# Five kept parts of wq instead of four, and four zero pieces moved earlier, in a two-layer decode step with its gradients

## The chip, the cores and the metric

The kernel runs on one core of a Trainium2 chip. The metric is the device time of one execution in microseconds (us). A core has five engines with their own instruction queues: PE (TensorE, matrix products; its weight loads are shown apart as PEld), DVE (VectorE), ACT (ScalarE), POOL (GpSimd) and SP (SyncE, which here does nothing but issue transfers). They work from on-chip memory (SBUF; PE writes to a second one, PSUM) and meet through semaphores. Transfers between HBM and SBUF are done by 16 DMA engines that all queues share. In this kernel SP issues every load of a weight and every store of a weight gradient (the profile's queue q1), and POOL issues the transfers that fill the untouched part of two outputs with zeros (queue q0).

## The reference, cut to what matters

One token passes through four blocks, A, B, A, B: A is attention over the last 4096 of 32768 cached keys and values (32 query heads, 4 key/value heads of 128), B is an MLP with the Mish activation. Both A blocks share the weights `wq` (1024 x 4096) and `wo` (4096 x 1024), both B blocks share `w1` (1024 x 3584) and `w2` (3584 x 1024); everything is bf16. The outputs are the result and the gradients of x, of both caches, and of all weights.

```
x = x + A(layernorm(x)); x = x + B(layernorm(x))      # twice
A(n): q = n @ wq;  p = softmax(q k^T * 128**-0.5);  return (p v) @ wo
B(n): h = n @ w1 + b1;  return mish(h) @ w2
return out, gradients of x, k_cache, v_cache, wq, wo, w1, b1, w2 for grad_out
```

As there is one token, each weight gradient is a sum of two outer products (one for each layer), 7 to 8 MiB that are computed from two short vectors each and then written. The gradients of the caches are zero outside the last 4096 positions: 56 pieces of 1 MiB of zeros. One MiB is 1.05 MB, the unit of the profile.

## The kernel before, in words

The order of the work is written out by hand; nothing is scheduled. The stages that matter, with their place in the profiled execution:

1. Forward through both layers, and backward through layer 1 (until about 245 us). Weights that don't fit are loaded again for each layer.
2. In the backward pass of attention, `attn_bwd` runs over `wo` in eight parts (the gradient of the attention output) and then over `wq` in eight parts (the gradient of the normed input; the program calls it `dn`). A part is a tile of 128 x 4096, 1 MiB. To multiply by it the other way round than it lies in memory, each of its four blocks of 128 x 1024 is turned: eight transposes on PE into PSUM (L482), and one copy back into the same place on ACT (L309) or DVE (L306), whichever is less loaded by a running count (`evac`). Then eight products with one column (L501) follow. To balance the engines, block 0 of the parts 2 to 7 isn't turned: DVE multiplies it with a broadcast vector and sums (`rowdot`, L459).
3. In layer 1's pass over `wq` (215 to 243 us), the parts named by `KEEP_Q2` stay in SBUF after they have been turned; layer 0's pass uses them again (`turned_q`), without a load and without transposes.
4. `w2`'s second pass (245 to 275 us): seven parts, each used for the MLP's output of layer 1 (`out_rows`, L347) and for the gradient of the hidden layer of layer 0.
5. `dn_b0` (275 to 285 us): the product with `w1`, which lies in SBUF (`W1`, shown as W). When it is done, W1's room is free: three slots of it are given to the ring (`ring.lend`), and other stretches take small rows that the last stage needs.
6. `attn_bwd` for layer 0: `wo` (285 to 305 us), the attention scores (305 to 315 us), `wq` (315 to 334 us).
7. The last stage (from 334 us): the weight gradients and the caches' gradients as outer products, PE into PSUM (L1063, L1114), copied to SBUF by ACT and DVE, and stored by SP in pieces of 0.375 to 1 MiB. Four outputs are filled in turns, so four buffers of 1 MiB fill at the same time; the first four may be stored by halves.

**The ring.** Streamed parts go through a ring of eight slots. The list of wanted loads is fixed at the start; `pump` issues the next one, on SP, as soon as a slot is free, and never out of order. A slot is given back by `release`, which the loops call through `later`, so that it comes after the products of the part have been issued; for `w2` that is while the next part is being worked on. A kept part of `wq` holds its slot from layer 1's pass until layer 0's. So with four kept parts, four slots serve `w2` and `wo` until `lend` adds three.

**The zeros.** `zeros(n, after)` issues n pieces from the zeroed tile `zt` on POOL. With `after`, POOL first copies one element of that tile, so the transfer cannot start before that tile is computed. Calls stand all over the backward pass, so that the zeros run beside work that doesn't fill the DMA engines; when the 56 pieces are used up, further calls do nothing. In layer 0's `attn_bwd` the hooks are `do1` (within the pass over `wo`, by part), `dp1` (after the first half of the scores), `dq1`, and `dn1` (within the pass over `wq`). `do1` at part 5 also issues small POOL transfers that put GA and GB into rows (L1025), `do1` at part 6 two more (L869); `twins` (L1055, on SP) copies rows to a second place, from which the last stage's products read.

The functions that the change touches, and what calls them:

Of the kernel before, what the change touches and what calls it, by code (L numbers as in the profile page):

```python
# [23 lines left out]
TD = D // P  # L24
# [69 lines left out]
def kernel(  # L94
# [136 lines left out]
    def want_q(k, ts=range(8)):  # L231
        for t in ts:
            ring.want(("q", k, t), wq_v[:, t, :], [P, J])

    def want_o(k, cs=range(8), homes=()):
        for c in cs:
            own = homes[c].rearrange("p (k d) -> p k d", k=4) if c < len(homes) else None
            ring.want(("o", k, c), wo_v[:, c], [P, 4, D], own, [("K", c)] if own is not None else [])
# [18 lines left out]
    def zeros(n, after=None):  # L257

        if after is not None and zjobs:
            nc.gpsimd.tensor_copy(pz[0:1, pz_n[0] % 16:pz_n[0] % 16 + 1], after[0:1, 0:1])  # L260
            pz_n[0] += 1
        for _ in range(n):
            if zjobs:
                dst = zjobs.pop()
                nc.gpsimd.dma_start(dst, zt[:])  # L265


    KEEP_Q = (5, 6, 7)
    KEEP_Q2 = (4, 5, 6, 7)
    EARLY_2 = (0, 1)  # L270
    MID_2 = (2, 3)
    W1S = W1[:].rearrange("p t f -> p (t f)")
# [17 lines left out]
    want_o(3)  # L290
    want_q(3, [t for t in range(8) if t not in KEEP_Q2])
    ring.pump()
# [4 lines left out]
    def even():  # L297
        load["D"] = load["A"] = max(load.values())
# [196 lines left out]
    def mv_open():  # L495

        fresh[0] = True
# [397 lines left out]
    def attn_bwd(l, sv, g, wo_key, wq_key, wq_keep, hooks, beside=None):  # L895
        name = f"A{l}"
        nc.vector.tensor_copy(GA[:, :, l], g[:])
        bcast(lambda c: GA[:, c, l:l + 1], TD)
        do32 = tmp([P, HQ], FP32, "da")
        mv_open()  # L900
        even()
        for c in range(8):
            ch = ring.get((*wo_key, c))

            behind[0] = max(2, 6 - max(0, c - DENSE + 1))
            rows_chunk(ch, c, GA, l, LB[0], do32, DA, 0 if c < DENSE else 1, None, (*wo_key, c))
            later(lambda c=c: ring.release((*wo_key, c)))
            hooks["do"](c)
        flush()
        for x, n0, k0 in ((0, DENSE, 0), (DENSE, 8, 1)):  # L910
            nc.vector.tensor_copy(do32[:, 4 * x:4 * n0].rearrange("p (c k) -> p c k", k=4)[:, :, k0:],
                                  TP[:, DA + 4 * x:DA + 4 * n0].rearrange("p (c k) -> p c k", k=4)[:, :, k0:])
        do_n = from_fours(do32[:])
        dov = DOC[:].rearrange("p v (g u l h) -> p v g u l h", g=G, u=2, l=2)
        do4 = do_n.rearrange("p (g h) -> p g h", g=G)
        nc.vector.tensor_copy(dov[:, 0, :, 0, l, :], do4)
        nc.gpsimd.tensor_copy(dov[:, 1, :, 1, l, :], dov[:, 0, :, 0, l, :])
        pr = small[:, 64:128]
        prv = pr[:].rearrange("p (g u h) -> p g u h", g=G, u=2)
        o4 = sv["o32"][:].rearrange("p (g h) -> p g h", g=G)  # L920
        for u in range(2):
            nc.vector.scalar_tensor_tensor(out=prv[:, :, u, :], in0=do4, scalar=float(D), in1=o4, op0=ALU.mult, op1=ALU.mult)
        sdp = small[:, 224:288]
        pxv = PX[:].rearrange("p (b l h) -> p b l h", l=2, h=8)
        dsv = DSX[:].rearrange("p (b l h) -> p b l h", l=2, h=8)
        for i in range(2):
            for t in range(16 * i, 16 * i + 16):
                for g_ in range(G):
                    c = scol(g_, t) - 512 * i
                    nc.tensor.matmul(SC[i][:, c:c + 8], lhsT=VS[:, g_, t, :],  # L930
                                     rhs=DOC[:, 0, g_ * 32 + l * 8:g_ * 32 + l * 8 + 8], start=True, stop=True)
            if i == 0:
                nc.tensor.matmul(TP[:, 320:384], lhsT=onesD[:], rhs=pr[:], start=True, stop=True)
                nc.vector.tensor_copy(sdp[:], TP[:, 320:384])
            s = SC[i].rearrange("p (tp c) -> p tp c", c=64)
            nc.vector.tensor_tensor(out=s, in0=s, in1=sdp[:, None, :].to_broadcast([P, 8, 64]), op=ALU.subtract)
            nc.vector.tensor_tensor(out=dsv[:, i * 64:(i + 1) * 64, l, :], in0=SC[i].rearrange("p (b h) -> p b h", h=8),
                                    in1=pxv[:, i * 64:(i + 1) * 64, l, :], op=ALU.mult)
        even()
        hooks["dp"]()  # L940
        dq_ps = MV[:, 320:320 + HQ]
        for i in range(2):
            for g_ in range(G):
                for t in range(16 * i, 16 * i + 16):
                    c = pcol(g_, t, l)
                    nc.tensor.matmul(dq_ps[:, g_ * 8:g_ * 8 + 8], lhsT=KT[:, g_, t, :], rhs=DSX[:, c:c + 8],
                                     start=(g_ == 0 and t == 0), stop=(t == TS - 1), skip_group_check=True)
        nc.vector.tensor_scalar(out=DQC[:, :, l], in0=dq_ps, scalar1=scale, scalar2=None, op0=ALU.mult)
        bcast(lambda c: DQC[:, c, l:l + 1], TD)
        even()  # L950
        hooks["dq"]()
        mv_open()
        bigs.append(SC[1])
        nc.vector.memset(dnp[:, 0:DENSE], 0.0)
        for t in range(TD):
            key = (*wq_key, t)
            ch = ring.get(key)
            nr = 0 if t < DENSE else 1
            behind[0] = max(2, 6 - max(0, t - DENSE + 1))
            if nr:  # L960
                rowdot(ch[:, 0:D], LB[0:1], D, dnp[:, t:t + 1])
            for k in range(nr, 4):
                h0 = 8 * k
                w = ch[:, h0 * P:(h0 + 8) * P]
                f = lambda w=w, h0=h0, t=t, k=k: mv(w, 8, TP[:, t:t + 1], lambda i: DQC[:, h0 + i, l:l + 1], k == 3)
                if key in turned_q:
                    later(f, True)
                else:
                    turned(w, 8, f)
            if t in wq_keep:  # L970
                ring.keep(key, ("q", 3, t))
                turned_q.add(("q", 3, t))
            else:
                later(lambda key=key: ring.release(key))
            hooks["dn"](t)
        flush()
        bigs.remove(SC[1])
        if beside is None:
            return ln_head(dnp, sv["n32"], sv["rstd"], g, name)
        return ln_bwd(dnp, sv["n32"], sv["rstd"], g, name, beside)  # L980

    turned_q = set()
# [13 lines left out]
    def dq3():  # L996
        zeros(3, DQC[:, 0, 1:2])

    g2 = attn_bwd(1, sA1, g3, ("o", 1), ("q", 2), KEEP_Q2,
                  dict(do=lambda c: conv(2 if 1 < c < 6 else 1), dp=dp3, dq=dq3, dn=lambda t: None),  # L1000
# [16 lines left out]
    def rowize(cols, n, base, off, queue):  # L1017

        b = big().bitcast(BF16)
        nc.tensor.transpose(b[0:2 * n, 0:P], cols[:].rearrange("p n l -> p (n l)"), ident_bf[:])  # L1020
        k = rt_n[0]
        rt_n[0] += 1
        nc.scalar.copy(rt[0:2 * n, k, :], b[0:2 * n, 0:P])
        for l in range(2):
            queue.dma_start(ROWS[base + l:base + l + 1, off:off + n * P].rearrange("o (t p) -> o t p", p=P),  # L1025
                            rt[l:2 * n:2, k, :])
# [118 lines left out]
    for c in range(7):  # L1145
        ch = ring.get(("2", 1, c))
        out_rows(ch, c, TF, lambda fb: AC[:, fb, 1:2])
        flush()
        rows_chunk(ch, c, GB, 0, LB[0], da0, DA, 2 if c else 0, "A" if c else None, ("2", 1, c))
        later(lambda c=c: ring.release(("2", 1, c)))  # L1150
        if c in (2, 4):
            zeros(1, da0[:, 4 * c:4 * c + 1])
    flush()
    bigs.remove(SC[1])
# [17 lines left out]
    def do1(c):  # L1172
        if c == 1:
            take_back("AC", 96, NOFF)
            take_back("OC", 32, NOFF)
            take_back("NB", 64, 0)
            take_back("NA", 0, 0)
        if c == 4:
            y = to_eight(YR, RT.rearrange("p a t s -> p (a t s)")[:, 0:512].bitcast(FP32))
            nc.vector.tensor_tensor(out=x4[:], in0=y, in1=x3[:], op=ALU.add)  # L1180
        if c == 5:
            rowize(GA, TD, 32, 0, nc.gpsimd)
            rowize(GB, TD, 96, 0, nc.gpsimd)
        if c == 6:
            rowize_f()

    def dp1():
        zeros(6)
        twins((96, NOFF + F), (32, NOFF + J), (64, NOFF + F))
        stage_free.extendleft(VS[:, g].rearrange("p t d -> p (t d)") for g in range(G))  # L1190

# [71 lines left out]
```

## Time and profile before

| | |
|---|---|
| median of 3 runs | 452.16 us (451.93 to 452.18) |
| profiled execution | 453.02 us, of which the span from first to last instruction is 451.2 us |
| busy: PE, PEld, DVE, ACT, POOL | 314.0, 242.7, 261.4, 209.2, 44.3 us |
| moved by DMA | 181.40 MB, mean 402 GB/s |
| of this the zeros' queue (q0) | 58.79 MB |
| of this SP's queue (q1) | 121.78 MB |

The page's rows of 40 slices (11.3 us each) give the busy share of each engine in tenths and the GB/s that the DMA engines moved. An answer by windows gives the same for chosen stretches: busy time and number of instructions of each engine, granted PE clock, DMA share and GB/s. In a timeline, a row is start, duration, engine, line, operation, tiles and count, and in brackets the idle time before it and what ended that. SPq and POOL rows with DMA_DIRECT2D are issues, not the transfers; "to landing" is the time from the issue to the last byte.

### The profile page before, as it was taken

To read this page: it belongs to the slowest core of one execution; us is meant where nothing else is said; L and a number is where in the kernel's file an instruction comes from. 1 tells how busy PE (TensorE), PEld (TensorE's weight loads), DVE (VectorE), ACT (ScalarE), POOL (GpSimd) and SP (SyncE) were. 2 spreads that over 40 slices of the span, in tenths; PEclk is the share of its full clock that TensorE was granted. 3 is DMA by queue.
4 is the path that set the end of the run, shared out by engine and by line. 5 is a ranking of instruction groups with operands and counts; after the bars stand their busy time and mean duration, and the time that the engine had idled before them with its cause. 6 is when DMAs were issued, how large, how long until landed. Compare 5 with 4: busy or idle time off the path is not lost.

```text
span 451.2 us, 12837 instructions
## 1 busy us (share of the span) xinstructions
PE 314.0 (70%) x5681; PEld 242.7 (54%) x5681; DVE 261.4 (58%) x516; ACT 209.2 (46%) x238; POOL 44.3 (10%) x95
## 2 busy tenths in 40 slices
PE   3835542556599798986797567988977888889500
PEld 3735542435576597986796455978852232235200
DVE  4504746376551663764276556773488989998400
ACT  2501101011058566772084631580448999998500
POOL 1000000000314212102100001124030000000000
PEclk9955555565559798896599956895665555555555
DMA  8999999989999999999999999998999999999995
GB/s 335 423 420 419 417 420 419 419 314 413 395 420 419 413 411 412 401 405 422 421 424 425 423 415 364 390 416 335 401 401 415 413 421 419 418 420 414 406 409 232
DMA packets 28425, 181.40 MB, mean 402 GB/s; under 512 B 3882, under 2 KB 4038, under 8 KB 9938
## 3 DMA queue, kind: packets, MB, share of 16 engines
q1 hardware_dynamic: 19862, 121.78, 66.1%
q0 software_dynamic: 8416, 58.79, 32.0%
q8 instruction: 44, 0.72, 0.6%
q14 instruction: 11, 0.09, 0.0%
q10 hardware_dynamic: 92, 0.02, 0.0%
HBM read 81.84 MB, written 98.62 MB: 400 GB/s over the span
## 4 chain that ended last, share of the span: by engine, by line
DMA 35%; PE 34%; DVE 14%; issue 5%; ACT 5%; POOL 0%; ACTq 0%; SPq 0%; DVEq 0%
DMA ring<-in_B_w_dram 13%; PE BIG L482 10%; DMA ring<-in_A_wq_dram 5%; DMA W<-in_A_wo_dram 4%; DMA out_dram<-zt 4%; DMA W<-in_B_w_dram 4%; PE TP L501 4%; PE wide L1114 4%; DVE junk L459 3%; PE BIG L660 3%; ACT ring L309 3%; DVE ring L306 3%; DMA out_dram<-KT 3%; DMA W<-in_A_k_cache_dram 2%; PE wide L1063 2%
## 5 line engine op out<-in xcount | busy, mean ns | idle before, releaser
L309 ACT COPY ring<-BIG 128x1024 bf16<-128x1024 bf16 x52 | 51.5, 1014 | 52.5 <-PE BIG L482 48.1
L1063 PE MATMUL wide<-W 2*128 2x512 bf16 x240 | 53.2, 597 | 9.0 <-ACT ring L309 2.4
L482 PE MATMUL BIG<-ident_bf,ring 128*128 128x128 bf16 x672 | 55.9, 238 | 3.2 <-issue 2.7
L482 PEld LDWEIGHTS <-ring 128*128 128x128 bf16 x768 | 53.1, 109 | 4.5 <-issue 3.9
L459 DVE CUSTOM_DVE_ANT_0 junk<-ring,SC 128x1024 bf16<-128x1024 bf16 x32 | 38.9, 1215 | 9.9 <-DMA ring<-in_B_w_dram 9.5
L1063 PEld LDWEIGHTS <-W 2*128 2x128 bf16 x240 | 12.6, 102 | 45.7 <-issue 44.6
L501 PEld LDWEIGHTS <-ring 128*128 128x128 bf16 x864 | 30.0, 98 | 12.2 <-issue 7.1
L309 ACT CAST ring<-wide 128x1024 bf16<-128x1024 f32 (+1 forms) x37 | 34.5, 1017 | 1.1 <-PE wide L1063 1.1
L265 POOL DMA_DIRECT2D out_dram<-zt x56 | 29.8, 535 | 35.2 <-DMA out_dram<-zt 34.2
L306 DVE CAST ring<-wide 128x1024 bf16<-128x1024 f32 (+1 forms) x27 | 31.3, 1198 | 2.8 <-PE wide L1063 2.8
L309 ACT COPY KT<-BIG 128x1024 bf16<-128x1024 bf16 x22 | 21.7, 1008 | 22.2 <-PE BIG L660 20.2
L306 DVE COPY ring<-BIG 128x1024 bf16<-128x1024 bf16 x32 | 21.8, 689 | 16.5 <-PE BIG L482 13.4
L459 DVE CUSTOM_DVE_ANT_0 junk<-ring,DSX 128x1024 bf16<-128x1024 bf16 x24 | 29.4, 1224 | 0.8
L482 PE MATMUL BIG<-ident_bf,W 128*128 128x128 bf16 x280 | 23.9, 234 | 1.2 <-issue 0.9
L544 PE MATMUL MV<-NA,ring 128*128 128x1 bf16 x512 | 15.1, 165 | 12.4 <-DMA ring<-in_A_wq_dram 11.0
L309 ACT COPY W<-BIG 128x1024 bf16<-128x1024 bf16 x20 | 19.8, 1016 | 7.8 <-PE BIG L482 7.7
L544 PEld LDWEIGHTS <-ring 128*128 128x128 bf16 x512 | 14.6, 103 | 13.1 <-DMA ring<-in_A_wq_dram 11.7
L1114 PE MATMUL wide<-W 32*128 32x256 bf16 x128 | 19.7, 403 | 1.5 <-DVE KT L306 0.9
L482 PEld LDWEIGHTS <-W 128*128 128x128 bf16 x288 | 19.2, 113 | 2.0 <-issue 2.0
L309 ACT CAST KT<-wide 128x1024 bf16<-128x1024 f32 x19 | 19.1, 1031 | 1.6 <-PE wide L1114 1.1
L347 PE MATMUL YR<-ring,AC 128*32 128x256 bf16 x208 | 10.6, 358 | 12.9 <-DMA ring<-in_B_w_dram 10.5
L309 ACT CAST W<-wide 128x1024 bf16<-128x1024 f32 x16 | 16.0, 1025 | 6.6 <-PE wide L1063 6.2
(280 smaller groups left out, 527.0 us busy)
## 6 DMA issues: line engine op xcount, KB each, us to landing
out_dram<-zt POOLq DMA_DIRECT2D x56, 1024.0 KB, 20.0
ring<-in_A_wq_dram SPq DMA_DIRECT2D x24, 1024.0 KB, 13.2
ring<-in_A_wo_dram SPq DMA_DIRECT2D x14, 1024.0 KB, 19.6
ring<-in_B_w_dram SPq DMA_DIRECT2D x13, 1024.0 KB, 19.7
W<-in_A_wo_dram SPq DMA_DIRECT2D x10, 1024.0 KB, 15.9
out_dram<-ring SPq DMA_DIRECT2D x8, 1024.0 KB, 13.9
W<-in_B_w_dram SPq DMA_DIRECT2D x8, 896.0 KB, 17.7
W<-in_A_k_cache_dram SPq DMA_DIRECT2D x4, 1024.0 KB, 9.0
```

The costliest lines, as they stand in the source:

```text
L265: nc.gpsimd.dma_start(dst, zt[:])
L306: nc.vector.tensor_copy(dst, src)
L309: nc.scalar.copy(dst, src)
L347: nc.tensor.matmul(bank[32 * j:32 * j + 32, 0:n].rearrange("p (g a) -> p g a", a=m.shape[-1]), lhsT=vec.to_broadcast([P, 32]), rhs=m, star ...
L459: nc.vector.tensor_tensor_reduce(out=out, in0=a, in1=vec, scale=1.0, scalar=acc if i else 0.0, op0=ALU.mult, op1=ALU.add, accum_out=acc)
L482: nc.tensor.transpose(b[:, i * P:(i + 1) * P], block(w, i) if block else w[:, i * P:(i + 1) * P], ident_bf[:])
L501: nc.tensor.matmul(out, lhsT=w[:, i * P:(i + 1) * P], rhs=rhs_of(i), start=fresh[0], stop=last and i == n - 1, skip_group_check=True)
L544: nc.tensor.matmul(q_ps[:, h:h + 1], lhsT=ch[:, h * P:(h + 1) * P], rhs=NA[:, t, l:l + 1], start=(k == 0 and h == 0), stop=(k == TD - 1), ...
L660: nc.tensor.transpose(b[:, i * P:(i + 1) * P], T[:, g, 8 * b8 + i, :], ident_bf[:])
L1063: nc.tensor.matmul(b[:, 512 * i:512 * i + 512], lhsT=R[at:at + 2, lo:lo + P], rhs=R[at:at + 2, ro + 512 * i:ro + 512 * i + 512], start=Tru ...
L1114: nc.tensor.matmul(b[:, k * 256:(k + 1) * 256], lhsT=RT[32 * g:32 * g + 32, a, tp, :], rhs=YS[32 * g:32 * g + 32, :], start=True, stop=Tru ...
```

## The change

`KEEP_Q2` gets part 3 as well, so five parts stay in the ring between layer 1's pass over `wq` and layer 0's, and layer 0 loads three parts. Layer 0's pass takes kept and loaded parts in turns (3, 0, 4, 1, 5, 2, 6, 7 instead of 0 to 7; layer 1's order is as before, as nothing is kept then); its hooks count steps, not parts. `w2`'s pass issues one piece of zeros at parts 1, 2, 4 and 5 instead of 2 and 4. `do1` at part 5 issues two pieces after its small transfers, and `dp1` four instead of six. As there are 56 pieces in all, the last call, after layer 0's `wq` pass (`zeros(2, ...t2)`), finds none left.

```diff
-    KEEP_Q2 = (4, 5, 6, 7)
+    KEEP_Q2 = (3, 4, 5, 6, 7)
...
-        for t in range(TD):
+        kept = [t for t in range(TD) if (*wq_key, t) in turned_q]
+        got = [t for t in range(TD) if t not in kept]
+        order = [x for i in range(TD) for x in kept[i:i + 1] + got[i:i + 1]]
+        for i, t in enumerate(order):
             key = (*wq_key, t)
             ch = ring.get(key)
             nr = 0 if t < DENSE else 1
...
-            hooks["dn"](t)
+            hooks["dn"](i)
...
-        if c in (2, 4):
+        if c in (1, 2, 4, 5):
             zeros(1, da0[:, 4 * c:4 * c + 1])
...
         if c == 5:
             rowize(GA, TD, 32, 0, nc.gpsimd)
             rowize(GB, TD, 96, 0, nc.gpsimd)
+            zeros(2)
...
     def dp1():
-        zeros(6)
+        zeros(4)
```

## The prediction

> **What bounds the kernel now.** I read the page's slices first, then the same by chosen stretches, then the DMA queues and the timelines of SP and POOL. The slices:
>
> ```profile
> DMA  8999999989999999999999999998999999999995
> GB/s 335 423 420 419 417 420 419 419 314 413 395 420 419 413 411 412 401 405 422 421 424 425 423 415 364 390 416 335 401 401 415 413 421 419 418 420 414 406 409 232
> ```
>
> The DMA engines are busy from end to end, at about 415 GB/s, with a few dips. By stretches:
>
> ```profile
> core 0: us, PE busy (x) PEld busy (x) DVE busy (x) ACT busy (x) POOL busy (x), PEclk, DMA share, GB/s
> 228.60:250.00 21.40, 17.95 (x425) 16.56 (x423) 15.72 (x33) 13.34 (x14) 0.71 (x2) 1.00 1.01 424
> 250.00:275.00 25.00, 15.64 (x269) 12.51 (x265) 12.82 (x24) 11.56 (x12) 1.48 (x5) 0.67 1.01 417
> 275.00:280.00 5.00, 4.86 (x100) 3.62 (x100) 4.12 (x12) 0.00 (x0) 1.17 (x3) 0.58 0.95 300
> 280.00:305.00 25.00, 21.14 (x437) 19.84 (x430) 18.13 (x43) 15.89 (x18) 5.55 (x10) 0.93 1.02 405
> 305.00:310.00 5.00, 4.05 (x131) 3.90 (x129) 1.93 (x9) 0.00 (x0) 3.42 (x7) 0.65 0.68 259
> 310.00:338.00 28.00, 23.93 (x497) 20.93 (x495) 16.60 (x30) 10.19 (x12) 6.09 (x15) 0.62 1.01 400
> 338.00:424.00 86.00, 73.77 (x395) 26.46 (x393) 76.54 (x76) 80.39 (x90) 0.00 (x0) 0.50 1.01 416
> 424.00:446.40 22.40, 0.00 (x0) 0.00 (x0) 0.00 (x0) 0.52 (x1) 0.00 (x0) 0.50 1.00 400
> ```
>
> From 424 to 446.4 us no engine works and the stores still drain at 400 GB/s. So the end is set by bytes: all that must be moved, plus the time in which the DMA engines had too little to do. Two such holes lie near the change: 275 to 280 us (300 GB/s) and 305 to 310 us (259 GB/s).
>
> How the two queues share, by queue in windows: the first two rows are 230 to 250 us, the third is 310 to 330 us, the last is from the first store, 338.3 us, to 360 us.
>
> ```profile
> q0 software_dynamic: 584, 4.22, 50.4%
> q1 hardware_dynamic: 577, 4.20, 50.0%
> ...
> q0 software_dynamic: 1081, 7.86, 98.4%
> ...
> q0 software_dynamic: 677, 4.87, 54.3%
> ```
>
> With zeros and loads both waiting, each gets half: 4.2 MB in 20 us, 5.0 us for a piece of 1.05 MB. Alone, zeros get everything. At the first store 4.87 MB of zeros are still to be moved.
>
> **The change part by part.**
>
> *One load less.* 1.05 MB at the 417 GB/s of 250 to 275 us: 2.5 us off the bytes.
>
> *Three slots for w2.* SP's issues:
>
> ```profile
> 228.64 6.40 SPq L71 DMA_DIRECT2D ring<-in_B_w_dram  x4
> 249.84 6.09 SPq L71 DMA_DIRECT2D ring<-in_B_w_dram  x3
> 261.65 13.12 SPq L71 DMA_DIRECT2D ring<-in_A_wo_dram  x4
> 280.24 1.72 SPq L71 DMA_DIRECT2D W<-in_A_wo_dram  x3
> 292.07 4.47 SPq L71 DMA_DIRECT2D ring<-in_A_wq_dram  x3
> 297.70 0.33 SPq L71 DMA_DIRECT2D W<-in_A_wq_dram  x1
> ```
>
> The chain, and the waits of PE in the pass:
>
> ```profile
> 234.71 19.52 DMA ring<-in_B_w_dram
> 254.28 0.62 PE YR L347 x16
> 255.60 13.85 DMA ring<-in_B_w_dram
> 269.49 1.04 PE YR L347 x12
> ...
> PE YR L347 <- DMA ring<-in_B_w_dram: 7.2, 4, 3.6
> ```
>
> Parts 0 to 3 of w2 are issued by 234.7 us into the four free slots; 4 to 6 wait for the release of 0 to 2, from 249.84 us on. PE waits for each of parts 3 to 6, 7.2 us in sum, so this pass already runs at the pace of its loads. With three slots, part 3 takes the issue at 249.84 us, 15 us later, and each later load moves back by one release. Zeros hold the other half of the DMA time, so part 3 needs 5.0 us of transfer plus a start. The start isn't shown alone; I bound it by 1 us and by 4 us (a lone zero piece, below, lands 6.6 us after its issue, of which 2.5 us is its transfer), and take 2 us, as SP's issue needs less than POOL's. Part 3 then lands at 256.8 us instead of 254.3: 2.5 us late (1.5 to 4.5). Before, parts 3 to 6 were 15.2 us apart in all, 5.1 us each, which is the half rate already; I add 0.5 us for the thinner queue. The pass ends 3.0 us later.
>
> *Two more zeros beside w2's pass.* 2.1 MB are now moved ahead of the last parts of `wo`: 5.1 us, less the hole at 275 to 280 us, which they fill: (417 - 300) x 5 / 417 = 1.4 us. So the last part of `wo` lands 3.7 us later; PE is busy for 21.14 of 25 us there, so the pass has little to wait with. I take 3.5 us for the end of the pass over `wo` (1.5 to 6). Behind it on POOL nothing waits: its next issues need ACT's copies.
>
> *Two zeros from dp1 to wo's part 5.* POOL:
>
> ```profile
> 299.01 2.06 POOL L1025 DMA_DIRECT2D W<-W  x4 [14.86 <-ACT W L1023]
> 303.20 1.00 POOL L869 DMA_DIRECT2D W<-W  x2 [2.13 <-ACT W L867]
> 306.77 3.21 POOL L265 DMA_DIRECT2D out_dram<-zt  x6
> ```
>
> Before, nothing big is issued between the last load of `wq` (297.7 us) and the zeros at 306.77 us; the loads run out and leave the hole at 305 to 310 us. Two pieces issued after the first row fill it: (414 - 259) x 5 / 414 = 1.9 us. The L869 transfers now queue behind 2.1 MB; `twins` waits for them on SP, but DQC's rows, next on SP, only come with DQC, about 13 us later.
>
> *The pass over wq.* It loses three turned blocks: 24 transposes, three copies, no product.
>
> ```profile
> 315.70:334.70 19.00, 15.72 (x326) 15.24 (x325) 12.15 (x22) 7.63 (x9) 3.33 (x10) 0.68 1.02 405
> L482 PE MATMUL BIG<-ident_bf,ring 128*128 128x128 bf16 x72 | 7.5, 277 | 1.0 <-issue 1.0
> 333.11 1.22 DVE L459 CUSTOM_DVE_ANT_0 junk<-ring,SC 128x1024 bf16<-128x1024 bf16 x1
> 316.12 2.08 SPq L1025 DMA_DIRECT2D W<-W  x2
> 322.77 3.19 SPq L1055 DMA_DIRECT2D W<-W  x2
> W<-W SPq DMA_DIRECT2D x4, 9.0 KB, 6.2
> ```
>
> 24 of 72 transposes are 2.5 us of PE's 7.5, and the order in turns spreads DVE's dots, whose last ends the pass now. But the last stage's first product reads the second copy of DQC's rows, issued until 326.0 us and landing 6.2 us later, at 332.2 us, against 334.7 us when the stage starts now. So the gain is between 0 and 2.5 us; I take the middle, 1.2. The last stage starts 3.5 - 1.2 = 2.3 us later.
>
> *The end.* Stores in the last stage:
>
> ```profile
> 338.30 2.94 SPq L1040 DMA_DIRECT2D out_dram<-W  x3
> 342.80 4.24 SPq L1035 DMA_DIRECT2D out_dram<-W  x3
> 350.75 0.33 SPq L1035 DMA_DIRECT2D out_dram<-ring  x1
> ```
>
> ACT and DVE make 166 copies in 86 us, 0.52 us each, up to 256 KiB a copy. The first four buffers go out early, 3.9 MiB (4.1 MB); the next four are full after 32 copies, at about 353 us with the small work between. From 338.3 to 353 us the DMA engines could move 14.7 x 0.414 = 6.1 MB, so 2.0 MB of zeros must bridge it. Afterwards copies (39.85 MB in some 90 us) outrun the DMA engines.
>
> *The sum,* against the profiled 453.0 us. By bytes: 453.0 - 2.5 - 1.4 - 1.9 + 0.5 (w2's thinner queue) = 447.7. Zeros left at 338.3 us: 4.87 - 1.05 - (1.4 + 1.9 - 0.5) x 0.414 = 2.65 MB; at the new first store, 2.3 us later, 1.7 MB: 0.3 MB too few, 0.7 us. **448.4 us.** The same from the other side: first store 340.6 + bridge 2.0 / 0.414 = 4.8 + stores 39.85 / 0.414 = 96.3 + 6.7 from the last transfers to the end (453.0 - 446.3) = 448.4. The profiled execution is 0.9 us above the median, so 447.5 us.
>
> **A rule weighed.** Landing of POOL's zeros, first those issued at 275.2 us, then those at 306.8 us:
>
> ```profile
> DMA to landing us min/median/max: 10.2/12.5/14.9
> ...
> DMA to landing us min/median/max: 6.6/11.8/17.3
> ```
>
> Both met DMA engines with time to spare, but beside a DVE that is busy 4.12 of 5 us the first piece took 10.2 us, beside one busy 1.93 of 5 us 6.6 us. The Trainium skill, SBUF — State Buffer, section "SBUF: two separate sides", says that a DMA issued from GpSimd gets its descriptors late while DVE holds the port they share, and only appears to be blocked. The trace fits that without proving it; what it would do here is the second rival.
>
> **The rivals.**
>
> 1. *The delay wins (slower).* With three slots only two loads are in flight; if each needs the 13.85 us of the chain's last one, parts come 6.9 us apart instead of 5.1: 4 x 1.8 = 7.2, with part 3's 2.5 us 9.7 us late, and the last stage 8.5 us late. Once zeros run out the time is 446.1 us plus this delay, so it decides from 6.9 us on; at 8.5 us it is 454.6, 453.7 against the median. For it: the four waits. Against it: those 13.85 us are mostly time in queue behind other loads, which three slots shorten.
> 2. *The holes stay.* Zeros moved beside a busy DVE start 3.6 us later (10.2 - 6.6) and miss the holes of 5 us. Only the load counts: 453.0 - 2.5 + 0.5 = 451.0, 450.1 against the median. Against it: the added zeros at w2's parts stand in a queue that isn't empty.
> 3. *It cancels.* The mechanism of the first with a delay of 6 to 7.8 us: 452.1 to 453.9, the time of before.
>
> **How the numbers follow.** Forecast 0.54 (446 to 450), first rival 0.21, second 0.17, third 0.08. Faster takes the forecast and the second: 0.71 and a little of the third, 0.72; 0.2% is about what a measurement here can tell from no change. The low end is the bytes with both holes filled and nothing new, 453.0 - 5.8 - 0.9 = 446.3, and 0.3 for zeros that mix with loads (424 GB/s, not 400): 446.0. The high end cuts off the worst half of the first rival: 453.7.
>
> **What would show it.** DMA moved about 180.35 MB; part 3 of w2 issued near 250 us; no slice under 390 GB/s from 275 to 310 us; the pass over `wo` ending near 308.5 us, the last stage starting near 337 us; less than 2 MB of zeros beside the first stores. The prediction is wrong if the last stage starts after 341 us, or if a hole of more than 2 us opens in w2's pass.

## The result, and the profile after

The changed kernel takes 451.35 us (median of 20 runs, 449.92 to 453.25) where the kernel before takes 452.35 us (20 runs, 451.63 to 454.07): a ratio of 0.9979, 95% interval 0.9969 to 0.9989. A second set gave 451.06 us and 0.9972 (0.9963 to 0.9982). The forecast was 447.5 us, 4.7 us below the time before; 1.0 us came, 1.3 us in the second set.

The first profiled execution of the changed kernel took 449.92 us (span 448.1 us), the fastest of its 20. The page's rows for the DMA engines, in 40 slices:

```profile
DMA  8999999989999999999999999999999899999995
GB/s 332 420 421 418 419 420 419 419 318 424 391 421 421 424 420 417 397 420 420 424 423 421 426 411 378 405 387 409 415 409 415 339 414 420 418 417 414 404 408 200
DMA packets 28281, 180.35 MB, mean 402 GB/s; under 512 B 3866, under 2 KB 4022, under 8 KB 9922
```

The 1.05 MB are saved. The dip that lay at 305 to 310 us is gone; a new one, 339 GB/s, lies at 347 to 358 us, beside the first stores. Two slices, 269 to 280 and 291 to 302 us, are under the 390 GB/s that the prediction named as a sign, at 378 and 387 GB/s. By chosen stretches (length, busy time of PE, PEld, DVE, ACT, POOL, granted PE clock, DMA share, GB/s):

```profile
239.20:275.80 36.60, 20.41 (x352) 16.41 (x352) 16.51 (x31) 13.58 (x14) 3.52 (x11) 0.64 1.01 412
275.80:285.30 9.50, 7.43 (x124) 5.86 (x125) 7.57 (x29) 0.33 (x1) 3.74 (x7) 0.68 1.00 392
285.30:309.80 24.50, 20.44 (x419) 19.42 (x418) 15.53 (x31) 15.64 (x18) 4.19 (x8) 0.90 1.00 396
305.00:310.00 5.00, 3.42 (x75) 2.92 (x73) 3.00 (x10) 3.13 (x4) 2.03 (x4) 1.00 1.02 416
317.70:336.40 18.70, 14.45 (x310) 13.50 (x310) 10.28 (x21) 7.63 (x9) 4.94 (x12) 0.77 1.01 410
...
350.00:357.50 7.50, 6.27 (x31) 1.69 (x31) 7.33 (x8) 7.29 (x10) 0.00 (x0) 0.50 0.74 301
426.00:442.50 16.50, 0.00 (x0) 0.00 (x0) 0.00 (x0) 0.02 (x1) 0.00 (x0) 0.50 1.00 399
442.50:446.40 3.90, 0.00 (x0) 0.00 (x0) 0.00 (x0) 0.00 (x0) 0.00 (x0) 0.50 0.07 29
```

The first row is `w2`'s pass, 36.6 us. Before, it took 29.7 us, and the last transfers drained like this:

```profile
245.20:274.90 29.70, 19.38 (x352) 15.47 (x352) 16.53 (x30) 13.58 (x14) 2.12 (x6) 0.73 1.01 419
446.00:449.50 3.50, 0.00 (x0) 0.00 (x0) 0.00 (x0) 0.00 (x0) 0.00 (x0) 0.50 0.16 64
```

In the rows of the changed kernel the third is the pass over `wo`, the fifth the one over `wq`. From 350 to 357.5 us the DMA engines lose 7.5 x (1 - 301/414) = 2.0 us. And the last row matters most: in the last 3.9 us of the transfers a share of 0.07 is at work, 29 GB/s. One engine of sixteen is 0.0625, and 1/16 of 414 GB/s is 26. So but for the first moments fifteen DMA engines have finished, and the end waits for one. Before, it was two to three engines on average in the last 3.5 us (a share of 0.16).

PE in `w2`'s pass, first the sum of its waits, then the longest in the timeline, and SP's issue of the part waited for:

```profile
PE YR L347 <- DMA ring<-in_B_w_dram: 13.8, 5, 7.0
```

```profile
254.53 1.04 PE L347 MATMUL YR<-ring,AC 128*32 128x256 bf16 x16 [7.02 <-DMA ring<-in_B_w_dram]
```

```profile
243.79 0.33 SPq L71 DMA_DIRECT2D ring<-in_B_w_dram  x1
```

Part 3 is issued 4.6 us after the start of the pass, as the fifth load was before, and PE has it 10.7 us later. SP's queue had all but run empty by then. The queues from 244.5 to 247 us:

```profile
q0 software_dynamic: 145, 1.06, 100.6%
q1 hardware_dynamic: 2, 0.00, 0.0%
```

Counted over the packets and landings of the trace, the first bytes of part 3 move at 247.4 us, 3.6 us after the issue; fifteen of its sixteen landings are there by 253.2 us, another 5.8 us, and the last comes at 254.5 us, 1.3 us behind them. The last part, by the chain of waits:

```profile
261.05 9.27 DMA ring<-in_B_w_dram
270.32 0.04 issue
270.37 1.04 PE YR L347 x15
```

### The profile page after: what moved, and what is told of

It reads as the page before. It is cut to its first block, busy times and chain, and to the rows that moved or that the text cites. A ratio compares the mean times of both kernels' runs of the same rounds, so it can differ in the third digit from the quotient of the medians.

```text
span 448.1 us, 12781 instructions
## 1 busy us (share of the span) xinstructions
PE 310.9 (69%) x5657; PEld 239.5 (53%) x5657; DVE 260.1 (58%) x513; ACT 209.2 (47%) x238; POOL 44.6 (10%) x96
## 4 chain that ended last, share of the span: by engine, by line
DMA 40%; PE 32%; DVE 11%; ACT 6%; issue 5%; SPq 0%; ACTq 0%; DVEq 0%
DMA ring<-in_B_w_dram 15%; PE BIG L482 9%; DMA W<-in_A_wo_dram 8%; DMA ring<-in_A_wq_dram 7%; DMA ring<-in_A_wo_dram 5%; PE TP L501 5%; DMA W<-in_B_w_dram 4%; PE wide L1117 4%; ACT ring L309 3%; PE wide L1066 3%; DVE ring L306 3%; DMA W<-in_A_k_cache_dram 2%; DVE W L306 2%; PE SC L347 2%; PE BIG L660 2%
## 5 line engine op out<-in xcount | busy, mean ns | idle before, releaser
L309 ACT COPY ring<-BIG 128x1024 bf16<-128x1024 bf16 x48 | 47.4, 1014 | 53.8 <-PE BIG L482 49.9
L482 PE MATMUL BIG<-ident_bf,ring 128*128 128x128 bf16 x624 | 50.6, 234 | 1.9 <-issue 0.9
L482 PEld LDWEIGHTS <-ring 128*128 128x128 bf16 x712 | 47.8, 107 | 3.6 <-issue 3.0
L501 PEld LDWEIGHTS <-ring 128*128 128x128 bf16 x832 | 28.7, 97 | 12.4 <-issue 8.2
L309 ACT COPY KT<-BIG 128x1024 bf16<-128x1024 bf16 x22 | 21.8, 1008 | 21.5 <-PE BIG L660 19.2
L309 ACT COPY W<-BIG 128x1024 bf16<-128x1024 bf16 x23 | 22.7, 1014 | 13.0 <-PE BIG L482 12.9
L306 DVE COPY ring<-BIG 128x1024 bf16<-128x1024 bf16 x30 | 20.4, 689 | 14.3 <-PE BIG L482 11.0
L482 PE MATMUL BIG<-ident_bf,W 128*128 128x128 bf16 x312 | 26.4, 238 | 3.1 <-DMA W<-in_A_wo_dram 2.2
L482 PEld LDWEIGHTS <-W 128*128 128x128 bf16 x320 | 21.5, 115 | 3.3 <-DMA W<-in_A_wo_dram 2.3
L544 PEld LDWEIGHTS <-ring 128*128 128x128 bf16 x512 | 14.6, 103 | 13.3 <-DMA ring<-in_A_wq_dram 11.9
## 6 DMA issues: line engine op xcount, KB each, us to landing
ring<-in_A_wo_dram SPq DMA_DIRECT2D x14, 1024.0 KB, 14.6
```

The lines of the kernel that those rows point to most:

```text
L306: nc.vector.tensor_copy(dst, src)
L309: nc.scalar.copy(dst, src)
L482: nc.tensor.transpose(b[:, i * P:(i + 1) * P], block(w, i) if block else w[:, i * P:(i + 1) * P], ident_bf[:])
L501: nc.tensor.matmul(out, lhsT=w[:, i * P:(i + 1) * P], rhs=rhs_of(i), start=fresh[0], stop=last and i == n - 1, skip_group_check=True)
L544: nc.tensor.matmul(q_ps[:, h:h + 1], lhsT=ch[:, h * P:(h + 1) * P], rhs=NA[:, t, l:l + 1], start=(k == 0 and h == 0), stop=(k == TD - 1), ...
```

## The experiments

Medians, each against the kernel before on the same chip:

| run | what differs | us (runs) | ratio to before |
|---|---|---|---|
| slots | changed, zeros where they were | 455.53 (6) | 1.0072 (1.0058 to 1.0086) |
| zeros | before, zeros moved | 452.24 (12) | 1.0000 (0.9992 to 1.0008) |
| hold | before, three slots for w2 | 453.75 (12) | 1.0037 (1.0021 to 1.0053) |
| flush | changed, slots released early | 450.40 (6) | 0.9962 (0.9949 to 0.9974) |
| flush_b | the same again | 450.44 (6) | 0.9957 (0.9942 to 0.9973) |
| flush2 | flush, two zeros beside w2 | 451.00 (6) | 0.9968 (0.9957 to 0.9979) |
| early | before, slots released early | 452.49 (12) | 1.0002 (0.9994 to 1.0011) |
| again | changed | 451.06 (11) | 0.9972 (0.9963 to 0.9982) |
| last | changed, kept parts last | 451.48 (12) | 0.9980 (0.9970 to 0.9989) |
| late2 | changed, wo's two zeros put back | 451.65 (12) | 0.9992 (0.9978 to 1.0006) |
| drop | before, the last zero piece left unwritten | 450.03 (6) | 0.9939 (0.9926 to 0.9953) |
| hw | flush2, 15 zeros issued by SP | 453.60 (12) | 1.0014 (0.9996 to 1.0031) |

### The two halves apart: five kept alone, zeros alone

`slots` is the changed kernel without the moved zeros, `zeros` the kernel before with them:

```diff
 # slots, against the changed kernel
-        if c in (1, 2, 4, 5):
+        if c in (2, 4):
...
-            zeros(2)
...
-        zeros(4)
+        zeros(6)
```

> The changed kernel with the zeros where they were before (parts 2 and 4 of w2, six in dp1, two at the end): five parts kept and parts in turns alone. Theory S (slots: a part of w2 is given back only after the next part's product on PE, which waits for that part's load, so with three slots the load queue runs empty) expects w2's pass, 29.7 us long before and 36.6 us after, to be 34 to 37 us, PE waiting 11 us or more for w2 in it. Rival Z (the two more zeros take the loads' half of the DMA engines) expects 30 to 32 us. With zeros in plenty for the last stage, S expects the time at bytes less the load plus new holes, 450.5 us (449.8 to 451.2); Z expects 449.5 us.

> The kernel before with the zeros moved as in the change (one more at parts 1 and 5 of w2, two at part 5 of wo, four in dp1, none at the end), four parts kept, order 0 to 7. S expects w2's pass at 30 to 32 us, PE waiting 7 to 9 us for w2, and the holes at 275 to 280 and 305 to 310 us smaller: 450.5 us (449.5 to 451.5). Z expects the pass at 35 to 37 us and 452 us or more.

Measured: 455.53 us for `slots`, 452.24 us for `zeros`. Both miss the 450.5 us expected, so neither theory had the time right; the passes are those of theory S. In `slots` PE waits about as long as in the changed kernel, and the DMA engines wait with it:

```profile
PE YR L347 <- DMA ring<-in_B_w_dram: 13.1, 4, 6.5
```

```profile
242.10:278.80 36.70, 20.45 (x352) 16.29 (x352) 16.51 (x30) 13.58 (x14) 2.12 (x6) 0.67 0.89 346
```

The pass is 36.7 us, as in the changed kernel, with 36.7 x (1 - 346/414) = 6.0 us of DMA time lost in it. `zeros` has a pass of 30.2 us:

```profile
242.60:272.80 30.20, 18.80 (x352) 15.28 (x352) 16.51 (x30) 13.58 (x14) 3.53 (x10) 0.78 1.01 425
```

So the long pass comes from having three slots instead of four, not from the zeros. The zeros gain nothing where there are four slots; where there are three they are worth 455.5 - 451.2 = 4.3 us, and `w2`'s pass moves 412 GB/s with them instead of 346. They cover a cost of the same change.

What `zeros` loses although no dip is left in its passes, by windows (the first stores, and the end):

```profile
341.00:357.00 16.00, 12.53 (x60) 3.46 (x58) 14.08 (x18) 14.42 (x19) 0.00 (x0) 0.50 0.84 339
442.00:448.60 6.60, 0.00 (x0) 0.00 (x0) 0.00 (x0) 0.00 (x0) 0.00 (x0) 0.50 0.28 112
```

Beside the first stores 16.0 x (1 - 339/414) = 2.9 us are lost, where zeros filled in before; and the last 6.6 us drain at 112 GB/s, on a few of the sixteen engines.

### Three slots without the saved load

```diff
+        ring.release("idle")
         ring.lend(lent)
...
+            elif key == ("q", 2, 3):
+                ring.keep(key, "idle")
```

> The kernel before, but part 3 of wq, though loaded again as before, holds its slot until the ring gets three more: w2 runs with three slots, no byte is saved, no zero moved. S expects w2's pass at 34 to 37 us and the time 1 to 3 us above before, 453.5 us, as the zeros at hand fill some of the empty queue; Z expects the pass at 30 us and the time of before.

453.75 us, 1.4 us more than before, as theory S had it; the single runs lie in two groups, eight from 452.5 to 453.8 us and four from 455.4 to 456.3 us. The profiled execution is of the second, with `w2`'s pass at 37.1 us. `slots` has that pass too and one load less, yet its median is higher than that of `hold`. The two differ in when the slot comes back (before `wo`'s pass here, in `wq`'s pass there) and in the bytes; what makes the first group of `hold` so fast wasn't profiled and stays open. That three slots instead of four cost time by themselves stands.

### The slot released before the wait for the next part

In `w2`'s pass the release of part c - 1 is carried out by `flush`, which stands after the products of part c (`out_rows`). In PE's queue the last products of part c - 1 stand behind those of part c, so the release waits for the landing of part c, and in the changed kernel's pass never more than two loads are on their way. The edit:

```diff
         ch = ring.get(("2", 1, c))
+        flush()
         out_rows(ch, c, TF, lambda fb: AC[:, fb, 1:2])
-        flush()
```

> The changed kernel with one line moved in w2's pass: the products that are still open for part c-1 are put before part c's product on PE, so that part c-1's slot comes free without waiting for part c's load. S expects w2's pass 3 to 6 us shorter than the 36.6 us of the change, PE's wait for w2 at 7 to 10 us instead of 13.8, the third and later loads issued right after the parts before them, and the time 1.5 to 3.5 us below the change, 448 to 450 us. Z expects no more than 0.5 us.

> The changed kernel with early release (flush) a second time, on the chip on which the early release alone is measured, for a narrower interval: flush stood at 450.4 us (0.9962 of before), the changed kernel at 451.06 and 451.35 us (0.9972, 0.9979), one piece of zeros less at 450.0 us. If flush beats the changed kernel, its ratio stays under 0.9968 here, 450.1 to 450.9 us. If its six runs were lucky, it comes out at 451 us and more.

450.40 and 450.44 us: 0.6 to 1.0 us faster than the changed kernel, on two chips, and just above the 448 to 450 us expected. The intervals of the single sets overlap; the four intervals together put the gain at some 0.7 us, 0.1 to 1.2 (an estimate). The chain of `flush` in the pass, and its waits:

```profile
244.00 10.17 DMA ring<-in_B_w_dram
254.22 1.04 PE YR L347 x16
...
258.67 10.15 DMA ring<-in_B_w_dram
268.87 0.62 PE YR L347 x16
```

```profile
PE TP L501 <- ACT ring L309: 6.9, 13, 0.8
PE YR L347 <- DMA ring<-in_B_w_dram: 4.7, 4, 2.4
```

A part still needs 10.2 us and more from issue to landing. PE waits 4.7 us for loads instead of 13.8, but 6.9 us for ACT's copies instead of 0.8, as the products that need these copies now stand ahead of the wait for the load. Together that is 11.6 us instead of 14.6, and these 3.0 us are what the pass is shorter: it takes 33.7 us at 424 GB/s.

> The kernel before (four parts kept, zeros where they were), with the early release of w2's slots alone. If the order of release costs only where the slots are three, as the reading of flush has it (three slots, late release: w2's pass 36.6 us; early: 33.6 us), the pass stays within 1 us of 29.7 to 30.0 us and the time within 0.2% of 452.4 us, and what flush gains over the changed kernel is a cost of the third slot that it gives back. If early release is a gain of its own, the pass and the time of this kernel fall too, by 0.5 to 1 us: 451.5 to 451.9 us.

Early release with four slots: 452.49 us, no change; the pass is 29.7 us as before. Its waits:

```profile
PE TP L501 <- ACT ring L309: 8.0, 14, 0.8
PE YR L347 <- DMA ring<-in_B_w_dram: 1.8, 2, 1.2
```

Here the waits only change places: 9.8 us instead of 2.1 + 7.2 = 9.3 before. So early release isn't a gain of its own: in the changed kernel it gives back part of what the missing slot cost.

> Three slots for w2, the slot given back ahead of the wait for the next part, and only the two zeros beside w2's pass that the kernel before had; the two in wo's pass stay. If the order of release is what left the load queue empty, the pass over w2 loses under 2 us of DMA time (5.9 us with three slots and the old order of release), takes 31 to 33.5 us, the pass over wo is shorter again by some 4 us than with four zeros (24 to 26 us instead of 29.8 us), some 3 MB of zeros are left at the first store, and the time is 449 to 450 us. If two loads in flight are too few whatever the order, a hole of 4 to 6 us opens in w2's pass and the time is 453 to 455 us.

451.00 us. The pass takes 33.8 us, 0.3 us more than the most that was expected of early release; the pass over `wo` takes 22.0 us instead of 29.8, shorter than expected, and 3.8 MB of zeros are left at the first store. But 33.8 x (1 - 390/414) = 2.0 us of DMA time are lost in the pass and 9.4 x (1 - 326/414) = 2.0 us in `dn_b0` behind it, and the time isn't the 449 to 450 us expected. It is 0.6 us above `flush`, with overlapping intervals: the two further zeros beside `w2` gain little or nothing once the slots are released early.

### One piece of 1.05 MB less, by itself

```diff
     zjobs.reverse()
+    zjobs.pop(0)
```

> The kernel before, with its last piece of zeros (1.05 MB, one eighth of the zeros of a head group in out_3 at most) not written; nothing else moves. It prices the first term of the prediction's sum by itself, one piece of 1.05 MB less. If the time is bytes alone, with enough zeros left beside the first stores (5.0 MB, 4.0 MB with this edit), 2.5 us go: 449.8 us. If the kernel before was bound by its chain as well, less goes: 451 to 452.3 us. In the first case the rest of the change, which has the same saving, cost what the changed kernel is above 449.8 us, 1.3 to 1.5 us.

The last piece of zeros isn't written in this run. 450.03 us beside 452.54: 2.5 us, what the bytes are worth (2.1 to 3.3 by the interval). The change saves the same bytes and stands at 451.06 to 451.35 us: everything else in it costs 1.0 to 1.3 us by the medians, 1.5 to 1.8 by the ratios. `flush` is 0.4 us above `drop`, with overlapping intervals. And `drop` is that fast with a hole that no zeros fill:

```profile
300.00:308.00 8.00, 6.35 (x143) 5.72 (x141) 3.45 (x10) 3.92 (x5) 2.28 (x6) 0.86 0.41 160
```

By its area it is 8.0 x (1 - 160/414) = 4.9 us, more than the two holes that the change was to fill.

### The order in turns, and wo's zeros

```diff
-        order = [x for i in range(TD) for x in kept[i:i + 1] + got[i:i + 1]]
+        order = got + kept
```

> The changed kernel with the loaded parts of wq first and the five kept ones last, instead of in turns. If the order in turns spreads the DVE's dots, as the prediction had it (its share of the 1.2 us, at most 2.5 us), the pass over wq takes 19.4 to 21 us instead of 18.7 us and the time grows by about as much as the last stage starts later, since too few zeros are left to hide it: 452 to 453 us. If the second copy of DQC's rows or the broadcast is what the last stage waits for, the pass stays within 0.5 us of 18.7 us and the time at 451.4 us.

451.48 us beside 451.06 of the changed kernel, with intervals that overlap. The pass over `wq` of `last`:

```profile
320.17:338.83 18.66, 15.05 (x310) 14.31 (x310) 11.73 (x23) 5.80 (x7) 4.41 (x12) 0.68 1.01 419
```

It takes the 18.7 us that it takes in turns in the first profile. No gain of the order shows.

> The changed kernel with the two zeros of wo's part 5 put back behind the scores, where they were; the two beside w2's pass stay. By the prediction's working the hole at 305 to 310 us comes back (1.9 us) and the 0.7 us beside the first stores go: 452.5 us. If a hole filled there is paid back beside the first stores, as the trace of the changed kernel has it (2.1 us lost from 350 to 357.5 us), the hole of 1.9 us comes back, the loss beside the first stores goes to under 0.5 us, and the time stays within 0.5 us of 451.4 us.

The windows of `late2` at the old hole and beside the first stores:

```profile
342.80:358.00 15.20, 12.03 (x56) 3.31 (x56) 13.28 (x17) 13.81 (x17) 0.00 (x0) 0.50 1.01 408
306.00:312.00 6.00, 4.40 (x113) 3.90 (x110) 3.15 (x10) 3.12 (x4) 1.96 (x5) 0.94 0.75 297
```

The hole is back, the one beside the stores is closed, and the time is 451.65 us, 0.6 us above the changed kernel; the intervals (0.9978 to 1.0006, 0.9963 to 0.9982) just overlap. So the 1.9 us that the zeros filled in `wo`'s pass were mostly paid back beside the first stores.

### Where a typical execution loses more than the first profile shows

> The changed kernel, unchanged, profiled a second time. Its first profiled execution (449.9 us) was 1.4 us under its median (451.35 us). Reading one, the start of the last stage moves with the chain of PE and the stores wait for it, because too few zeros are left: this profile then shows the last stage starting 1 to 3 us later than 336.4 us, a stretch under 350 GB/s beside the first stores that is longer than before (3 us and more lost instead of 2.1), and the time some 451.3 us. Reading two, the difference is only in how the last transfers drain: the last stage starts within 0.5 us of 336.4 us, the loss beside the first stores stays near 2 us, and the DMA engines alone end later.

> The changed kernel, unchanged. Its two profiled executions (449.9 and 450.4 us) were among its fastest; its median is 451.06 to 451.35 us, with single executions up to 453.3 us, while flush (early release) has none above 451.5 us. Where does a typical execution lose its 1 us? If in the last stage, an execution of 451.5 us and more shows the last stage starting after 340 us and a stretch beside the first stores in which all sixteen DMA engines are idle. If in w2's pass, it shows a hole of more than 2 us there (under 350 GB/s), as with three slots and fewer zeros. If neither, both look as in the first two profiles and the difference lies in the last transfers.

`look2` and `look3` are further executions of the same kernel with the same readings. The five, and the two of `flush`; the rate is from the start of `w2`'s pass to the start of `wo`'s, and the loss is that against 423 GB/s:

| execution, us | w2's pass starts | GB/s to the start of wo's | lost, us | last stage starts |
|---|---|---|---|---|
| 449.92 (first) | 239.1 | 408 | 1.6 | 336.4 |
| 450.38 (again) | 240.0 | 403 | 2.1 | 339.9 |
| 450.80 (look2) | 240.8 | 392 | 3.3 | 338.1 |
| 451.18 (look3) | 241.3 | 391 | 3.4 | 341.0 |
| 451.59 (look1) | 244.5 | 366 | 6.1 | 338.2 |
| 450.19 (flush) | 239.3 | 422 | 0.1 | 339.6 |
| 450.23 (flush_b) | 239.6 | 423 | 0.0 | 339.6 |

The row of the slowest, `look1`:

```profile
244.47:289.87 45.40, 27.39 (x477) 22.04 (x478) 24.14 (x58) 14.04 (x15) 7.26 (x17) 0.69 0.96 366
```

Of the three readings it is the hole in `w2`'s pass: time and loss rise in the same order. The later the pass starts, the larger the hole, and the fewer zeros are still queued from earlier: in all five 35 pieces are issued ahead of the pass, and of these 36.7 MB queue q0 has 3.6, 3.6, 3.2, 3.1 and 2.3 MB left to move at its start, in the order of the table. The start of the last stage doesn't order the times. The loss grows by 4.5 us and the time by 1.7 us only; `look1` has no hole beside its stores (411 GB/s from 341.9 to 362 us, where the first profile drops to 301).

In `again` and `flush`, whose last stage starts after 339 us, the hole beside the first stores has this form (windows, `again` first):

```profile
357.00:358.70 1.70, 1.49 (x9) 0.41 (x7) 1.70 (x3) 1.68 (x3) 0.00 (x0) 0.50 0.06 24
```

```profile
356.50:358.60 2.10, 1.89 (x11) 0.55 (x9) 2.10 (x3) 1.91 (x3) 0.00 (x0) 0.50 0.06 25
```

One engine alone, while fifteen wait for stores. Both kernels then drain together, without the lone engine at the end. `flush` is the fastest version with the five kept parts although its hole beside the stores is among the largest (3.6 us at 414 GB/s). The landings say why: each of the last stores, from 426 to 442 us, has its sixteenth landing 3.3 us after the fifteenth in the first profile, but 0.3 us after it in `again` and 0.4 us in `flush`, where it was 2.2 to 3.5 us behind ahead of the hole. An engine that lags uses such a hole to catch up, and what it makes up there it needn't do at the end.

> The kernel before, unchanged, profiled a second time, as the changed kernel was. In its first profile the DMA engines did not end together: of the last 4.5 us one to four of sixteen were still at work. In the changed kernel's first profile one engine alone worked for the last 3 us, and at no moment after 140 us were all sixteen idle. If one engine carries more than the others, this profile shows the same: at the end a stretch of 3 to 5 us at 30 to 110 GB/s, the holes near 275 and 305 us with some engines at work all the time, and some 452.3 us. If that was chance, the last transfers end within 2 us of each other.

452.35 us, the time expected, 0.7 us under the first profile. The hole of the second profile, 299 to 309 us in 40 slices:

```profile
DMA  8999999989996553311221001111010110111039
GB/s 360 459 492 393 393 393 426 492 364 394 361 397 262 229 179 100 133 67 66 100 100 68 0 33 45 45 45 45 9 58 33 54 47 8 59 42 53 18 102 403
```

Here too one or two engines go on while the rest has nothing to do, and the end drains for 2.9 us at 143 GB/s. The pass over `wo` takes 26.5 us in this profile and 21.8 us in the first: between two executions of one kernel it moves by more than the change was forecast to move it.

### Who makes one engine lag

```diff
-            zeros(7, OC[:, 0, 1:2])
+            zeros(7, OC[:, 0, 1:2], nc.sync)
...
-    zeros(8, x3)
+    zeros(8, x3, nc.sync)
```

(with three arguments, `zeros` issues on the named engine and doesn't wait for a tile)

> The same kernel as flush2 (three slots, early release, two zeros beside w2's pass), but 15 pieces of zeros from 114 to 143 us are issued by SP instead of POOL. In all kernels the last of the sixteen landings of a transfer falls behind the others from about 140 us on, while POOL's queue alone is at work: 1 us behind at 134 us, 4 us at 165 us. If POOL's queue makes one engine slow, the lag at 165 us stays under 2 us, the last engine ends under 3 us behind the others (5 us in flush2), and the time is 448.5 to 450 us. If the lag comes from elsewhere (other work on that engine, whoever issues), it grows to 4 us by 165 us as before, and the time stays within 0.6 us of 451.0 us. If SP's loads are held up behind its own zeros, the pass over wq of the upper layer starts late and the time is above 452 us.

453.60 us, 2.6 us above `flush2`, and above the 452 us set for loads held up behind SP's own zeros; but the pass over `wq` of the upper layer starts when it does in `flush2` (216.3 and 216.6 us) and only ends later. In the profiled execution, one of its faster (451.90 us), `w2`'s pass starts at 247.2 us instead of 241.1 and has a hole of its own (the first row), and the end still drains over 4.8 us (the second):

```profile
247.00:278.00 31.00, 20.13 (x361) 15.76 (x358) 16.68 (x32) 13.60 (x14) 2.13 (x6) 0.86 0.89 335
444.00:448.80 4.80, 0.00 (x0) 0.00 (x0) 0.00 (x0) 0.00 (x0) 0.00 (x0) 0.50 0.28 113
```

It gives no answer. The pieces issued by SP land within 2.4 us until 158 us, as POOL's did at that time in the changed kernel (2.8 us). Then pieces of both queues are under way, and the last landing of SP's falls behind the fifteenth by 1.0 us at 164 us and 3.7 us at 191 us, that of POOL's by 0.6 and 1.9 us. So the lag isn't confined to what POOL issues, but 41 pieces were still POOL's, and they ran beside it.

## Why the prediction was wrong

It named the direction, and the time lies in its range, but the gain is about a quarter of the forecast. By its own steps:

- *One load less, 2.5 us.* Right: 2.5 us in `drop`.
- *Two holes filled, 1.4 and 1.9 us.* This step failed, and with it the sentence it stands on, that the end is set by the bytes and the time in which the DMA engines had too little to do. The holes were filled, the second whole (305 to 310 us at 416 GB/s), the first by about 0.9 of its 1.4 us (275.8 to 285.3 us at 392 GB/s). But `zeros`, which fills them without anything else, gains 0.0 us (0.9992 to 1.0008), and `drop` gains its full 2.5 us with a larger hole. The zeros taken from beside the first stores opened a hole there: the forecast charged 0.7 us for that; it is 2.0 us in the first profile, 2.9 in `zeros` and up to 3.6 in others. And a hole of the mean needn't be idle time of the engine that is last: it is from the landings that this is read, and no run sets the lag of one engine by itself. The working had a sign of it: the 6.7 us that it put between the last transfers and the end hold 3.2 us in which a few engines still moved bytes, until 449.5 us.
- *Part 3 of w2, 2.5 us late.* The step failed by its size. The place of the issue was right (4.6 us into the pass). From issue to landing I took 7.0 us, with 9.0 as the upper bound; it is 10.7 us: 3.6 us of start where 2 were taken, 5.8 us of transfer for fifteen engines where 5.0 were taken, and 1.3 us for the last engine, which the sum didn't have. So part 3 comes 6.2 us later in the pass instead of 2.5, and the pass is 6.9 us longer, not 3.0 (36.2 to 36.6 us in five profiles, 29.7 and 30.0 before). The 0.5 us for the thinner queue was right: from part 3 to the last part it is 15.8 us instead of 15.2. That only two loads are on their way stood in the first rival; that the release waits for the next part's landing stood nowhere in the sum.
- *The pass over wo, 3.5 us later.* Not to be judged: it takes 24.5 us beside 21.8 in the first profiles, 26.5 us in the second of before. Its end lies at 309.8 to 313.2 us in five profiles, at 306.3 and 307.2 before.
- *The pass over wq, 1.2 us shorter.* Near: 17.1 to 19.8 us, in the middle 19.3, against 20.4 and 19.8. The reason given, the order in turns, shows no part in it (`last`).
- *The last stage, 2.3 us later.* 336.4 to 341.0 us against 334.7 in both profiles of before: 1.7 to 6.3 us, in the middle 3.5.
- *From the profiled execution to the median, 0.9 us less.* Wrong. The second profile of before took 452.35 us, its median; the five of after reach from 1.4 us below its median to 0.2 above. What one execution lost was carried over to another kernel as if it were a property of the pair.

Put together from the runs: 452.4 (before) - 2.5 (bytes) + 0.0 (zeros with four slots) + 1.2 (the rest, which no run measures alone) = 451.1 us. Early release, which changes nothing but `w2`'s pass, gives back 0.6 to 1.0 of the rest, so most of it is the missing slot's cost.

Of the rivals, the delay (the first) had the cause right, three slots and two loads in flight, but not its form: the parts after part 3 come 5.3 us apart, not 6.9, and its 9.7 us weren't reached. The second, "only the load counts", gave 450.1 us, which is near, by a mechanism that the trace refutes: the zeros came in time and the holes closed. The third, the delay at 6 to 7.8 us, gave 452.1 to 453.9 us against the profiled execution, so 451.2 to 453.0 against the median. The measured 451.35 us lies in that by luck: the last stage starts only 1.7 to 6.3 us later. The sign of wrongness that was set down, a hole of over 2 us in `w2`'s pass, is met in the slower executions; the other, a last stage after 341 us, is just reached in `look3` (341.0). The hole: 36.2 x (1 - 376/414) = 3.3 us in `look1`, from this row:

```profile
244.50:280.70 36.20, 20.42 (x352) 16.25 (x352) 16.51 (x30) 13.58 (x14) 3.53 (x10) 0.67 0.97 376
```

## What to carry to other kernels

A dip in the mean rate of the DMA engines need not be worth its area: look at the last few us, and where they run at a sixteenth of the rate, one engine lags, and saved bytes are surer than filled dips. When a ring loses a slot, follow what the release itself waits for; behind the wait for the next part it leaves only two loads on their way with three slots, and moving it one line gave back 0.6 to 1.0 us. Where a load is issued into an empty queue, count the time until its first bytes as well. Price each part of a change of several alone: here one part only repaid what another cost.

## What the runs showed of the hardware

The sixteen DMA engines don't stay level. In the changed kernel and `flush` at least one was at work at every moment from 140 us to the end of the transfers, counted over all packets, while the mean had dips of 2 to 3.6 us; the last engine ended up to 4 us after the others. In the first profile of the changed kernel the first and the last landing of a zero piece are 2.0 to 2.2 us apart at 138 to 153 us, 3.7 us at 165 us and 5.6 us at 183 us, while POOL's queue alone is at work. From 332 to 343 us the last landing of a piece of zeros comes 2.2 to 4.0 us after the fifteenth in the first profile, `again` and `flush`, but 0.9 to 1.4 us in `slots` and at most 0.3 us in `hold`, whose holes no zeros filled. That holes cost time only once they have used up the lag fits these runs; it isn't tested by itself. The Trainium skill, DMA: Bandwidth & Descriptors, section "Latency and other measured facts", says that two engines, 7 and 15, are usually slower than the others, and gives the ports of the descriptor rings of GpSimd's path as its best guess, not certain. The trace agrees that one lags (it is alone at 24 to 29 GB/s, a sixteenth of the rate), but doesn't name it. It speaks against the guess as the whole cause: in the second profile of before, with only stores issued by SP under way, the last landing falls from 0.3 us behind the fifteenth at 362 us to 1.6 us behind it at 420 us.

A load of 1.05 MB on SP's queue, with zeros waiting on POOL's, took 9.3 to 10.7 us from issue to landing in `w2`'s pass (12.7 us where another load stood ahead of it), where at half the rate its bytes need 5.0 us. When SP's queue was empty, its first bytes moved 3.3 to 3.6 us after the issue (part 3 in `again`, `look1`, `flush` and the first profile).
